# The second MLP's first layer in pairs of token tiles: 512-column products that share a PSUM bank, and the leaky step as a maximum

## The chip, the cores and the metric

The kernel runs on one core of one Trainium2 chip. Its time is the device time of one execution in microseconds. A core has a matrix engine (TensorE, PE; its weight loads are PEld), a vector engine (VectorE, DVE), an activation engine (ScalarE, ACT), a general engine (GpSimd, POOL) and a queue that issues the transfers (SyncE, SP). Each takes its instructions in order and waits on semaphores for the others. PE writes only to PSUM, which has 8 banks of 512 float32 columns by 128 partitions.

## The reference

Linear attention over `q`, `k`, `v` gives 4608 tokens of 512 features. Two MLPs follow, each 512 -> 2048 -> 512. The change is in the first layer of the second one and in its leaky step:

```python
h = x @ w_in                                            # first MLP, squared ReLU
r = np.maximum(h, 0.0)
x = (r * r) @ w_out
h = x @ w2_in                                           # (4608 x 512) @ (512 x 2048)
g = np.maximum(h, 0.0) + alpha * np.minimum(h, 0.0)     # alpha: one per column, 0 to 0.3
out = g @ w2_out
```

The weights come as 8-byte numbers; the kernel joins their halves into float32.

## The kernel before

The tokens are cut into 9 tiles of 512 (`T`). Four stages follow each other, each over all tiles: the attention with the first layer of MLP 1 (`hidden_stage`, line 756), its second layer (`project_stage`, line 793), the first layer of MLP 2 (`hidden_pairs`, line 900), its second layer (`project_stage` again). Between stages the tiles lie in device memory (`r_dram`, `y_dram`).

Every float32 operand is split into a rounded head (ACT, `split.head`, line 481) and the rest (DVE, `split.rest`, line 484), both of type fp32r, and a product is made of three matmuls: `PAIRS = ((1, 0), (0, 1), (0, 0))`. From the second stage on, a 2 x 2 block product is formed from seven block products instead of eight (a scheme of Strassen's kind in Winograd's form): sums of operand blocks are made first (`token_blocks`, lines 500, 506, 509; `Pairs.made` for the weights), and sums of the seven results afterwards. In `hidden_pairs` a group `g` is 256 of the 2048 hidden columns against one tile, whose 512 tokens are two halves of 256 (`HALF`). Each of its seven products (1, 3, 2, 6, 7, 5, 4) is six matmuls of 256 columns: two 128-row halves of the contraction (`c`) by three pairs. They land in the halves of four banks. `prelu` adds them up: ACT copies products 1 and 3 out of PSUM (line 928), DVE makes the sums (lines 932, 935, 938, 944), POOL one of them (941), and the leaky step is ReLU(-z) on ACT (947), its scaling by `-alpha` (952), and max(z, 0) plus that, on DVE (955) for even groups or on ACT and POOL (967, 968) for odd ones. A store to `r_dram` (972) follows.

The order on each engine is not the order of the code. `Plan` collects all operations with an engine, an assumed cost, what they come after, the buffers they take and a due time, and places them one by one: on each engine, the operation that can start soonest, and among those within `SLACK` of it the one due first. The result is a fixed order per engine. Buffers have fixed places (`homes`, in units of 256 words), and kinds whose places overlap share them in time: the loaded token blocks `ri` (14 to 35), results `o` (37 to 53), and `z`, `zt` of the leaky step.

Around the change: the last tile of the second stage ends with `combine` (lines 825 to 841), which adds its seven accumulated banks on ACT and DVE and stores them (`store_y`). The weights of `w2_in`, 8 groups, are brought back from device memory and split (768 and 1024 elements a group) as soon as the second stage's last tile frees their places, so partly after the third stage has begun. The weights of `w2_out` and the first token blocks of the last stage are made in the same way during the last tile of the third.

## Time and profile before

| what | value |
| --- | --- |
| median of 3 runs | 1626.44 us (1624.84 to 1627.63) |
| span of the profiled execution | 1623.9 us |
| time of the profiled execution | not recorded beside its span; the median of the runs lies 2.5 us above the span |
| third stage, starts of the first and the last L900 matmul | 881.4 and 1253.6 us |
| matmuls of the third stage | 3024 of 128x128 by 256 columns |
| DMA over the span | 176 GB/s |

The page counts busy time per engine, follows back the chain of work that ended last, and lists groups of instructions by source line with their mean duration and the idle time ahead of them. Matmuls overlap in the pipeline: the mean duration of one is longer than the distance from one to the next, so the distance is taken from stretches of the chain that hold many of them.

### The profile page before, as it was taken

The numbers are of one execution on the slowest core, as the hardware profiler recorded it, in microseconds if no ns is written. First come the engines' busy times: TensorE is split into PE (matmuls) and PEld (weight loads), VectorE is DVE, ScalarE is ACT, GpSimd is POOL, SyncE is SP. The second block draws the span as 40 slices with busy tenths as digits, with TensorE's granted clock in tenths as the row PEclk, the third lists the DMA queues.
The fourth block names the chain that finished last, engine by engine and source line by source line (L and its number), as shares of the span: only waits on it lengthen the run. The fifth ranks groups of instructions, "written<-read, shape, count | busy, mean of one in ns | idle before, by whom it ended". The sixth has DMA issues, their size and how long they took to land.

```text
span 1623.9 us, 30239 instructions
## 1 busy us (share of the span) xinstructions
PE 1583.6 (98%) x11840; PEld 1489.6 (92%) x11840; DVE 1214.4 (75%) x2108; ACT 963.3 (59%) x1500; POOL 276.1 (17%) x248
## 2 busy tenths in 40 slices
PE   5899999999999999999999899999999999999998
PEld 3678888888888999999999899999999999999998
DVE  7765767667626888888877977777769998888873
ACT  5677766766757544444444777787778644444442
POOL 4431111111100000000021333333333000000011
PEclk9999999999999999999999999999999999999999
DMA  8677788887657444444444433333346544444441
GB/s 218 193 224 270 240 265 262 282 289 269 243 207 272 151 142 140 137 129 135 133 151 158 163 131 131 130 143 135 133 165 215 189 150 151 133 145 133 131 120 64
DMA packets 125247, 287.19 MB, mean 177 GB/s; under 512 B 15024, under 2 KB 73392, under 8 KB 125104
## 3 DMA queue, kind: packets, MB, share of 16 engines
q1 hardware_dynamic: 125104, 285.26, 53.3%
q8 instruction: 92, 1.51, 0.4%
q14 instruction: 51, 0.42, 0.1%
HBM read 168.83 MB, written 116.39 MB: 176 GB/s over the span
## 4 chain that ended last, share of the span: by engine, by line
PE 89%; DVE 5%; DMA 2%; issue 2%; ACT 1%; POOL 1%; SPq 0%; DVEq 0%; POOLq 0%; ACTq 0%
PE bank L793 43%; PE bank L756 23%; PE bank L900 19%; DVE sr L484 2%; PE bank L590 1%; DMA sb<-in_moe_w_in_dram 1%; PE bank L664 1%; PE bank L736 1%; PE bank L679 1%; PE bank L680 1%; PE bank L678 0%; DMA sb<-in_k_dram 0%; DVE sb L500 0%; DVE sb L932 0%; POOL sr L397 0%
## 5 line engine op out<-in xcount | busy, mean ns | idle before, releaser
L793 PE MATMUL bank<-sr 128*128 128x256 f32 x6048 | 727.5, 283 | 0.9 <-DVE sb L832 0.7
L793 PEld LDWEIGHTS bank<-sr 128*128 128x128 f32 x6048 | 726.3, 192 | 2.0 <-DVE sb L832 0.9
L481 ACT CAST sr<-sb 128x512 fp32r<-128x512 f32 (+2 forms) x534 | 371.6, 713 | 366.5 <-PE bank L793 216.0
L484 DVE TENSOR_TENSOR sr<-sb,sr 128x768 fp32r<-128x768 f32 (+2 forms) x534 | 426.6, 824 | 107.8 <-ACT sr L481 106.9
L756 PE MATMUL bank<-sr 128*128 128x512 f32 x1680 | 406.5, 397 | 5.8 <-POOL sr L397 5.8
L756 PEld LDWEIGHTS bank<-sr 128*128 128x128 f32 x1680 | 311.8, 189 | 72.5 <-POOL sr L397 7.4
L900 PE MATMUL bank<-sr 128*128 128x256 f32 x3024 | 366.4, 284 | 5.5 <-DVE sr L484 4.0
L900 PEld LDWEIGHTS bank<-sr 128*128 128x128 f32 x3024 | 364.9, 193 | 6.9 <-DVE sr L484 5.3
L506 POOL TENSOR_TENSOR sb<-sb 128x256 f32<-128x256 f32 x16 | 17.6, 1098 | 719.0 <-ACT sr L481 672.3
L784 ACT ACTIVATE sb<-bank 128x512 f32<-128x512 f32 x144 | 85.7, 595 | 76.7 <-PE bank L756 65.7
L500 DVE TENSOR_TENSOR sb<-sb 128x512 f32<-128x512 f32 x162 | 114.7, 710 | 3.3 <-DMA sb<-r 1.8
L968 POOL TENSOR_TENSOR sb<-sb 128x1024 f32<-128x1024 f32 x36 | 89.5, 2486 | 156.7 <-ACT sb L967 152.4
L947 ACT ACTIVATE sb<-sb 128x1024 f32<-128x1024 f32 x72 | 76.2, 1058 | 42.8 <-DVE sb L944 42.5
L832 DVE TENSOR_TENSOR sb<-sb,bank 128x512 f32<-128x512 f32 x108 | 71.1, 685 | 36.8 <-PE bank L793 17.1
L952 ACT ACTIVATE sb<-sb,al_neg 128x512 f32<-128x512 f32 x144 | 96.9, 717 | 2.2
L785 ACT ACTIVATE sb<-sb 128x512 f32<-128x512 f32 x144 | 91.0, 632 | 3.4
L932 DVE TENSOR_TENSOR sb<-bank,sb 128x512 f32<-128x512 f32 x72 | 49.4, 687 | 41.7 <-ACT sb L928 36.5
L660 POOL TENSOR_TENSOR sb<-sb 128x512 f32<-128x512 f32 x36 | 37.8, 1051 | 225.4 <-DVE sb L656 84.8
L941 POOL TENSOR_TENSOR sb<-sb 128x256 f32<-128x256 f32 x72 | 53.9, 750 | 104.4 <-DVE sb L932 100.0
L509 DVE TENSOR_TENSOR sb<-sb 128x256 f32<-128x256 f32 x146 | 64.3, 442 | 4.2
L938 DVE TENSOR_TENSOR sb<-bank,sb 128x512 f32<-128x512 f32 x72 | 49.8, 691 | 18.5 <-PE bank L900 13.1
L506 DVE TENSOR_TENSOR sb<-sb 128x256 f32<-128x256 f32 x146 | 63.0, 435 | 0.8
(67 smaller groups left out, 1055.5 us busy)
## 6 DMA issues: line engine op xcount, KB each, us to landing
r<-sb SPq DMA_DIRECT2D x144, 512.0 KB, 3.1
sb<-r SPq DMA_DIRECT2D x144, 512.0 KB, 3.7
j<-sb SPq DMA_DIRECT2D x24, 896.0 KB, 6.0
sb<-j SPq DMA_DIRECT2D x24, 896.0 KB, 5.0
sb<-in_moe_w_in_dram SPq DMA_DIRECT2D x32, 512.0 KB, 5.2
sb<-in_moe_w_out_dram SPq DMA_DIRECT2D x32, 512.0 KB, 4.9
y_scratch<-sb SPq DMA_DIRECT2D x36, 256.0 KB, 2.8
sb<-y_scratch SPq DMA_DIRECT2D x18, 512.0 KB, 4.9
```

The costliest lines, as they stand in the source:

```text
L481: nc.scalar.copy(of(parts.ap[:, :n]), what())
L484: nc.vector.tensor_tensor(of(parts.ap[:, n:]), what(), of(parts.ap[:, :n].bitcast(F32)), op=ALU.subtract)
L500: nc.vector.tensor_tensor(two(block(4, 2)), two(block(1, 2)), block(0).unsqueeze(1).to_broadcast([P, 2, HALF]), op=ALU.subtract)
L506: e.tensor_tensor(block(6), block(2), block(4), op=ALU.add)
L756: nc.tensor.matmul(h.ap, w[:, a, c, :], x_parts(x[c][0])[:, b, :], start=(c == 0 and n == 0), stop=(c == KB - 1 and n == 2),)
L784: o = plan.add(lambda: nc.scalar.activation(ro.ap[:, half], h.ap, AF.Relu), "act", 0.6, [o, even], new=new, use=[h, ro])
L785: return plan.add(lambda: nc.scalar.activation(ro.ap[:, half], ro.ap[:, half], AF.Square), "act", 0.63, [o], use=[ro])
L793: nc.tensor.matmul(target[:, m * HALF:(m + 1) * HALF], one[:, u, ms], two[:, w, :], start=start and m == 0 and i == 0, stop=stop and m == ...
L900: nc.tensor.matmul(h.ap[:, at * HALF:(at + 1) * HALF], a[:, u, c * P:(c + 1) * P], b[:, w, :], start=(m == 0 and c == 0 and z == 0), stop= ...
L947: nc.scalar.activation(zt.ap, block(0, 4), AF.Relu, scale=-1.0)
L952: nc.scalar.mul(half, half, al_neg[:, f:f + 1])
L968: o = plan.add(lambda: nc.gpsimd.tensor_tensor(block(0, 4), block(0, 4), zt.ap, op=ALU.add), "pool", 2.3, [o], use=[z, zt])
```

## The change

The third stage is `hidden_wide` instead of `hidden_pairs`. Eight of the nine tiles are taken in pairs, so that a block of tokens is a whole tile (512 columns, one bank) and the two blocks of a product are the two tiles; the ninth tile is taken alone with 256 columns as before. Each of the seven operands of a tile pair has a buffer of its own (`xt`, 14 in all: seven for each half of the contraction) and is made by one ACT copy and one DVE subtraction (`operand`, lines 924 to 928 of the new code). Two groups of weights are worked on together, their products alternating.

Products 1, 6, 7 and 4 add up in one bank: between them ACT copies the running sum out (`copy`, lines 1031 to 1042), and the next product goes on adding only after that. Product 2 has a bank, and 5 and 3 share one; DVE adds these to the copies (`plus`). The leaky step is one DVE operation, max(alpha * z, z) (`leak`), for alpha up to 1. For larger alphas `sign` turns the column round, and the rows of `w2_out` are turned back when they are joined (`rebias_by`). POOL has no part in the stage any more. `y_dram` is written so that a block of a tile pair can be read in pieces of 512.

```diff
-    al_neg = const.tile([P, NF], F32, name="al_neg")
+    sign = const.tile([P, NF], F32, name="sign")
+    rebias_by = const.tile([P, NF], F32, name="rebias_by")
...
-        z=kind(5 * HALF, 3, homes=homes(28, 5, 3)), zt=kind(4 * HALF, 2, homes=homes(43, 4, 2)),
+        xr=kind(7 * BANK, 2, homes=homes(14, 14, 2)), xt=kind(2 * BANK, 14, area=1, homes=homes(112, 4, 14)),
+        z=kind(2 * BANK, 8, homes=homes(49, -4, 2) + homes(8, -4, 3) + homes(38, -4, 7)),
...
-            nc.scalar.activation(high, high, AF.Prelu, scale=2.0 ** -112, alpha=-(2.0 ** 32))
+            scale = rebias_by[:, f:f + 1] if signed else 2.0 ** -112
+            nc.scalar.activation(high, high, AF.Prelu, scale=scale, alpha=-(2.0 ** 32))
...
+    def wide_blocks(load, after, n):
...
+        def operand(p, i, o):
+            x = buf(K["xt"])
+            operands[p] = x
+            o = plan.add(lambda: nc.scalar.copy(x.ap[:, :n], block(i)), "act", act_us(n), [o], new=[x], use=[j])
+            done[p] = plan.add(
+                lambda: nc.vector.tensor_tensor(x.ap[:, n:2 * n], block(i), x.ap[:, :n].bitcast(F32), op=ALU.subtract),
+                "dve", dve_us(n), [o], use=[x, j], lock=True,
+            )
...
+        sums = plan.add(t13, "dve", dve_us(2 * n), [loaded], use=[j], lock=True)
+        operand(1, 1, loaded)
+        operand(2, 3, loaded)
...
+    def hidden_wide(weights, y_done, r, gate):
...
+            for g in range(0, G, 2):
+                both = [Group(weights, xs, t, first, n, g + m, r) for m in range(2)]
+                for m, p in ((0, 1), (1, 1), (0, 2), (0, 6), (1, 6), (1, 2), (0, 5), (0, 7), (1, 7), (1, 5), (0, 4), (1, 4), (0, 3), (1, 3)):
+                    last[t, g + m] = both[m].product(p)
...
+            read = {6: 1, 7: 6, 4: 7, 3: 5}.get(p)
+            us = MM if n == BANK else MM2
+            o = product_op(
+                unit, 6 * us / MM, [self.weights.done[g][s], *(x[1][p] for x in self.xs), self.ends.get(read)],
+                new=[h] if start else [], use=[h, wb, *(x[0][p] for x in self.xs)],
+            )
...
+            def copy(to, by):
+                nc.scalar.mul(to, h.ap[:, :n], sign[:, by])
+
+            def plus(to, by):
+                nc.vector.scalar_tensor_tensor(to, h.ap[:, :n], sign[:, by], to, op0=ALU.mult, op1=ALU.add)
+
+            def leak(to, by):
+                nc.vector.scalar_tensor_tensor(to, to, al[:, by], to, op0=ALU.mult, op1=ALU.max)
...
-    h2, r2 = hidden_pairs(w2i, y_done, r_dram[1], lambda t, h2: p1[T - 1, 3, 5] if t == 0 else h2[t - 1, 1])
+    h2, r2 = hidden_wide(w2i, y_done, r_dram[1], lambda t, h2: p1[T - 1, 3, 5] if t == 0 else h2[t - 1, 3])
```

How the change moves instructions shows at three places. First PE where the second stage ends and the third begins; `bank5_70` and `bank3_68` hold products of the last tile of the second stage (L793 before, L796 now), six matmuls a row. Before:

```order
L793 MATMUL bank6_71<-sr_64 128x256 x6
L793 MATMUL bank2_67<-sr_64 128x256 x6
L793 MATMUL bank5_70<-sr_64 128x256 x6
L900 MATMUL bank4_69<-sr_64 128x256 x6
L793 MATMUL bank3_68<-sr_64 128x256 x6
L900 MATMUL bank7_72<-sr_64 128x256 x6
L900 MATMUL bank4_69<-sr_64 128x256 x6
L900 MATMUL bank7_72<-sr_64 128x256 x6
L900 MATMUL bank0_65<-sr_64 128x256 x6
L900 MATMUL bank1_66<-sr_64 128x256 x6
```

Now, from the same product on:

```order
L796 MATMUL bank6_71<-sr_64 128x256 x6
L796 MATMUL bank2_67<-sr_64 128x256 x6
L796 MATMUL bank5_70<-sr_64 128x256 x6
L796 MATMUL bank3_68<-sr_64 128x256 x6
L983 MATMUL bank4_69<-sr_64 128x512 x6
L983 MATMUL bank7_72<-sr_64 128x512 x6
L983 MATMUL bank0_65<-sr_64 128x512 x6
L983 MATMUL bank4_69<-sr_64 128x512 x6
L983 MATMUL bank1_66<-sr_64 128x512 x6
L983 MATMUL bank6_71<-sr_64 128x512 x6
L983 MATMUL bank7_72<-sr_64 128x512 x6
L983 MATMUL bank4_69<-sr_64 128x512 x6
```

The one product of the third stage that stood ahead of the second stage's last (product 5) is gone from there. The third stage begins behind it, and its products of two groups alternate; a bank comes back after two to four others.

Second, DVE at the same place. L832 before and L835 now are the additions of `combine`, which wait for PE's last products; L484 and L487 are `split.rest`; in the new code L895, L901 and L904 are the sums of token blocks and L911 is the DVE half of an operand. Before:

```order
L832 TENSOR_TENSOR sb_63<-sb_63,bank0_65 128x512
L832 TENSOR_TENSOR sb_63<-sb_63,bank6_71 128x512
L841 TENSOR_TENSOR sb_63<-sb_63 128x512
L832 TENSOR_TENSOR sb_63<-sb_63,bank2_67 128x512
L832 TENSOR_TENSOR sb_63<-sb_63,bank5_70 128x512
L484 TENSOR_TENSOR sr_64<-sb_63,sr_64 128x768
L832 TENSOR_TENSOR sb_63<-sb_63,bank3_68 128x512 x2
L932 TENSOR_TENSOR sb_63<-bank7_72,sb_63 128x2x256
L935 TENSOR_TENSOR sb_63<-bank0_65,sb_63 128x256
L484 TENSOR_TENSOR sr_64<-sb_63,sr_64 128x1024
```

Now:

```order
L835 TENSOR_TENSOR sb_63<-sb_63,bank0_65 128x512
L835 TENSOR_TENSOR sb_63<-sb_63,bank6_71 128x512
L844 TENSOR_TENSOR sb_63<-sb_63 128x512
L835 TENSOR_TENSOR sb_63<-sb_63,bank2_67 128x512
L835 TENSOR_TENSOR sb_63<-sb_63,bank5_70 128x512
L911 TENSOR_TENSOR sr_64<-sb_63,sr_64 128x512
L895 TENSOR_TENSOR sb_63<-sb_63 128x1024
L911 TENSOR_TENSOR sr_64<-sb_63,sr_64 128x512
L901 TENSOR_TENSOR sb_63<-sb_63 128x512
L911 TENSOR_TENSOR sr_64<-sb_63,sr_64 128x512
L835 TENSOR_TENSOR sb_63<-sb_63,bank3_68 128x512
L911 TENSOR_TENSOR sr_64<-sb_63,sr_64 128x512
```

The block sums of the second half of the contraction (the second L895) and the first operand made from it (the L911 behind it) stand behind four additions of `combine` and the sum of two of its results (L844).

Third, PE at the end of the third stage. Before, the products of the last stage (L793) follow those of the third:

```order
L900 MATMUL bank6_71<-sr_64 128x256 x6
L900 MATMUL bank1_66<-sr_64 128x256 x6
L900 MATMUL bank6_71<-sr_64 128x256 x6
L900 MATMUL bank3_68<-sr_64 128x256 x6
L900 MATMUL bank4_69<-sr_64 128x256 x12
L793 MATMUL bank5_70<-sr_64 128x256 x6
L793 MATMUL bank7_72<-sr_64 128x256 x6
L793 MATMUL bank0_65<-sr_64 128x256 x6
```

Now one product of the last stage (L796) stands ahead of the last seven products of the third:

```order
L983 MATMUL bank7_72<-sr_64 128x256 x6
L796 MATMUL bank6_71<-sr_64 128x256 x6
L983 MATMUL bank3_68<-sr_64 128x256 x6
L983 MATMUL bank5_70<-sr_64 128x256 x6
L983 MATMUL bank3_68<-sr_64 128x256 x6
L983 MATMUL bank5_70<-sr_64 128x256 x6
L983 MATMUL bank3_68<-sr_64 128x256 x6
L983 MATMUL bank1_66<-sr_64 128x256 x6
L983 MATMUL bank7_72<-sr_64 128x256 x6
L796 MATMUL bank2_67<-sr_64 128x256 x6
L796 MATMUL bank0_65<-sr_64 128x256 x6
```

## Rows read from the trace of the kernel before

**Rows 1.** The page: span, and PE's busy time with its share and instructions

```profile
span 1623.9 us, 30239 instructions
...
PE 1583.6 (98%) x11840; PEld 1489.6 (92%) x11840; DVE 1214.4 (75%) x2108; ACT 963.3 (59%) x1500; POOL 276.1 (17%) x248
```

**Rows 2.** The page: the chain that ended last, by engine and line

```profile
PE 89%; DVE 5%; DMA 2%; issue 2%; ACT 1%; POOL 1%; SPq 0%; DVEq 0%; POOLq 0%; ACTq 0%
```

**Rows 3.** Busy time, the third stage: PE, PEld, DVE, ACT, POOL, clock, DMA

```profile
934.00:1243.00 309.00, 308.94 (x2575) 308.74 (x2573) 224.58 (x371) 237.40 (x329) 119.04 (x91) 1.00 0.39 144
```

**Rows 4.** The chain in order of time: start, length, what, instructions

```profile
49.87 2.75 PE bank L756 x12
...
473.21 46.24 PE bank L756 x204
...
916.03 10.38 PE bank L900 x72
932.25 271.85 PE bank L900 x2262
```

**Rows 5.** PE in order of time, second stage into third; idle ahead in brackets

```profile
882.16 0.88 PE L793 MATMUL bank<-sr 128*128 128x256 f32 x6
...
916.03 14.08 PE L900 MATMUL bank<-sr 128*128 128x256 f32 x103 [3.18 <-DVE sr L484]
930.36 1.31 PE L900 MATMUL bank<-sr 128*128 128x256 f32 x6 [0.24 <-DVE sr L484]
932.25 12.98 PE L900 MATMUL bank<-sr 128*128 128x256 f32 x104 [0.58 <-DVE sr L484]
```

**Rows 6.** Busy time and granted clock of PE alone, 916 to 922 us

```profile
916.00:918.00 2.00, 1.97 (x9) 0.50 0.20 82
...
920.00:922.00 2.00, 2.00 (x19) 1.00 0.32 129
```

**Rows 7.** PE in order of time, third stage into fourth

```profile
1244.31 9.61 PE L900 MATMUL bank<-sr 128*128 128x256 f32 x78 [1.36 <-DVE sb L932]
...
1297.65 2.53 PE L793 MATMUL bank<-sr 128*128 128x256 f32 x19 [0.69 <-DVE sb L832]
```

**Rows 8.** DVE in order of time, around 1240 us

```profile
1240.73 2.92 DVE L500 TENSOR_TENSOR sb<-sb 128x512 f32<-128x512 f32 x1
1243.57 0.68 DVE L932 TENSOR_TENSOR sb<-bank,sb 128x512 f32<-128x512 f32 x1
```

**Rows 9.** POOL in order of time, around 1240 us

```profile
1240.70 2.41 POOL L968 TENSOR_TENSOR sb<-sb 128x1024 f32<-128x1024 f32 x1 [4.38 <-ACT sb L967]
```

**Rows 10.** Groups by line and shape, whole run, DVE and ACT: busy, mean ns

```profile
L484 DVE TENSOR_TENSOR sr<-sb,sr 128x512 fp32r<-128x512 f32 x324 | 222.0, 699 | 52.2 <-ACT sr L481 51.7
...
L484 DVE TENSOR_TENSOR sr<-sb,sr 128x768 fp32r<-128x768 f32 x186 | 182.7, 987 | 49.7 <-ACT sr L481 49.3
...
L952 ACT ACTIVATE sb<-sb,al_neg 128x512 f32<-128x512 f32 x144 | 96.9, 717 | 2.2
L785 ACT ACTIVATE sb<-sb 128x512 f32<-128x512 f32 x144 | 91.0, 632 | 3.4
...
L932 DVE TENSOR_TENSOR sb<-bank,sb 128x512 f32<-128x512 f32 x72 | 49.4, 687 | 41.7 <-ACT sb L928 36.5 <-PE bank L900 3.5 <-issue 1.6
...
L928 ACT COPY sb<-bank 128x512 f32<-128x512 f32 x72 | 41.3, 573 | 35.7 <-PE bank L900 30.2 <-POOL sb L968 3.1 <-DMA r<-sb 1.2
...
L935 DVE TENSOR_TENSOR sb<-bank,sb 128x256 f32<-128x256 f32 x72 | 30.5, 424 | 6.9 <-PE bank L900 0.5 <-POOL sb L968 0.2
...
L484 DVE TENSOR_TENSOR sr<-sb,sr 128x1024 fp32r<-128x1024 f32 x24 | 29.8, 1242 | 5.9 <-ACT sr L481 5.9
```

**Rows 11.** DVE in order of time, the second stage's end

```profile
880.98 0.69 DVE L841 TENSOR_TENSOR sb<-sb 128x512 f32<-128x512 f32 x1
881.78 1.48 DVE L832 TENSOR_TENSOR sb<-sb,bank 128x512 f32<-128x512 f32 x2
```

**Rows 12.** The page: transfers of y, KB each, us from issue to landing

```profile
y_scratch<-sb SPq DMA_DIRECT2D x36, 256.0 KB, 2.8
```

More of the change, by code (lines that the diff above doesn't have):

```diff
@@ L879, in store_out, with block, t13, t2 @@
         )
-    def hidden_pairs(weights, y_done, r, gate):
+    WIDE = [(t, BANK) for t in range(0, T - 1, 2)] + [(T - 1, HALF)]
+    def wide_blocks(load, after, n):
+        j = buf(K["xr"])
+        operands, done = {}, {}
+        def block(i, many=1):
+            return j.ap[:, i * n:(i + many) * n]
+        def t13():
+            nc.vector.tensor_tensor(
+                block(4, 2).rearrange("p (i n) -> p i n", i=2), block(1, 2).rearrange("p (i n) -> p i n", i=2),
+                block(0).unsqueeze(1).to_broadcast([P, 2, n]), op=ALU.subtract,
+            )
+        def t2():
+            nc.vector.tensor_tensor(block(6), block(2), block(4), op=ALU.add)
+        def t4():
+            nc.vector.tensor_tensor(block(0), block(3), block(6), op=ALU.subtract)
+        def operand(p, i, o):
[6 more added lines that the diff above has]
+            )
+        loaded = None
+        for h in range(2):
+            loaded = plan.add(
+                lambda h=h: load(block(0, 4).rearrange("p (k h t) -> p k h t", k=2, h=2)[:, :, h], h), "sp", ISSUE,
+                [*after, loaded], new=[] if h else [j], use=[j], mb=n / 1000,
+            )
+        sums = plan.add(t13, "dve", dve_us(2 * n), [loaded], use=[j], lock=True)
+        operand(1, 1, loaded)
+        operand(2, 3, loaded)
+        o = plan.add(t2, "dve", dve_us(n), [sums], use=[j], lock=True)
+        operand(6, 6, o)
+        operand(5, 4, sums)
+        operand(7, 5, sums)
+        o = plan.add(t4, "dve", dve_us(n), [o], use=[j], lock=True)
+        operand(4, 0, o)
+        operand(3, 2, loaded)
+        return operands, done
@@ L883, in hidden_pairs @@
+    def hidden_wide(weights, y_done, r, gate):
         last, stored = {}, {}
[L884 removed]
+        for t, (first, n) in enumerate(WIDE):
             xs = []
             for c in range(2):
[L887 to L911 removed]
@@ new lines, in load @@
+                def load(to, h, c=c, first=first, n=n):
+                    if n == BANK:
+                        y = y_dram[first + h].rearrange("p (k c h) t -> p k c (h t)", c=2, h=2)
+                        nc.sync.dma_start(to, y[:, :, c])
+                    else:
+                        y = y_dram[first].rearrange("p (k c h) t -> p k c h t", c=2, h=2)
+                        nc.sync.dma_start(to, y[:, :, c, h])
+                ys = [y_done[t2, i, j] for t2 in range(first, first + n // HALF) for i in (1, 2) for j in (1, 2)]
@@ new lines, in hidden_wide @@
+                xs.append(wide_blocks(load, [*ys, gate(t, last)], n))
+            for g in range(0, G, 2):
+                both = [Group(weights, xs, t, first, n, g + m, r) for m in range(2)]
+                for m, p in ((0, 1), (1, 1), (0, 2), (0, 6), (1, 6), (1, 2), (0, 5), (0, 7), (1, 7), (1, 5), (0, 4), (1, 4), (0, 3), (1, 3)):
+                    last[t, g + m] = both[m].product(p)
+                for m in range(2):
+                    for h in range(2):
+                        for t2 in range(first, first + n // HALF) if n == HALF else [first + h]:
+                            stored.setdefault((t2, g + m), []).append(both[m].stored[h])
```

172 lines of the change are left out of this document (86 added, 86 removed).

## The prediction

> **What bounds the kernel now.** I read the page first: PE is busy for 98% of the span [rows 1], and the chain that ended last is PE for 89% [rows 2]. Then the stretch of the third stage that lies free of its two ends: PE is busy for 308.94 of 309.00 us, while DVE has 224.6 (73%), ACT 237.4 (77%) and POOL 119.0 us (39%) [rows 3]. So in the middle of the stage nothing but PE's own pace counts, and a change of ACT's or DVE's work is worth nothing there by itself. The pace is in the chain in order of time [rows 4]: 2262 matmuls of 256 columns in 271.85 us, 0.1202 us from one to the next, and in the first stage 204 of 512 columns in 46.24 us, 0.2267 us. Both ran at the full granted clock. Two of 256 columns take 0.2404, one of 512 takes 0.2267: 0.0137 us is what a matmul costs beside its columns.
>
> At the ends PE waits. In order of time [rows 5] the second stage goes over into the third without a gap; then PE stands idle for 3.18 us before 916.03, and for 0.24 and 0.58 us soon after, each time for DVE's L484, the second half of a weight split. After the 3.18 us the granted clock was 0.50, half of 2.4 GHz, and full again by 920 [rows 6]; the 72 matmuls behind the gap took 10.38 us [rows 4] instead of 72 x 0.1202 = 8.65, so 1.73 us more. Two gaps of 1.36 and 0.69 us lie at the change to the fourth stage [rows 7]. The 1.36 us comes at the end of a DVE addition of 2.92 us [rows 8] that lay beside a POOL operation of 2.41 us [rows 9]; alone such an addition takes about 0.69.
>
> **The change, part by part.** *Matmuls.* Before: 3024 x 0.1202 = 363.4 us. Now four tile pairs x 8 groups x 42 = 1344 of 512 columns and 8 x 42 = 336 of 256: 1344 x 0.2267 + 336 x 0.1202 = 304.7 + 40.4 = 345.1 us. That is 18.3 us less. The rows give 0.2292 as the other end for 512 columns (12 in 2.75 us, an isolated product with its end [rows 4]); with it 3.4 us of the gain are lost. I take 0.2267, since products follow each other closely here as in the long row.
>
> On this term one rule stands against the trace. The Trainium skill (TensorE: Matmul & The Clock Gate, "Wait — 56ns, not 53.3ns?") gives the distance of warm matmuls as columns over 2.4 GHz and a fixed 2.5 ns; it was measured on another type. By it 1344 matmuls fewer would save 1344 x 2.5 ns = 3.4 us. The rows here show 13.7 ns and decide.
>
> *The late weights.* Groups of weights were used up every 42 x 0.1202 = 5.05 us, and DVE, which splits them, fell behind. A pair of groups now lasts 84 x 0.2267 = 19.0 us. The waits of 3.18 + 0.24 + 0.58 = 4.0 us and the 1.73 us at the low clock should go. Bounds: nothing to all of it stays. DVE's work in a wide tile: 8 groups x 7 operations on 512 columns (3 `plus`, 4 `leak`) x 0.687 = 38.5 us by L932; 14 operands x 0.699 = 9.8 by L484; sums 2 x (1.242 + 2 x 0.687) = 5.2; together 53.5 us [rows 10] beside 8 x 42 x 0.2267 = 76.2 us of PE. In the first tile up to 8 x (0.987 + 1.242) = 17.8 us of weight splits come on top: 71.3 of 76.2. It fits, closely, and by the order of DVE two of the eight groups and a part of the third are split before the stage begins.
>
> *A new wait at the stage's first product.* Product 1 needs operands of both halves of the contraction. In the order of DVE the second half's sum (second L895) and its first operand (L911) stand behind the additions of `combine`, of which the last needs product 4. In the trace that pair of additions began at 881.78, right behind L841, and lasted 1.48 us [rows 11], so to 883.26. Behind it come L911, L895 and L911: 0.70 + 1.24 + 0.70, less 0.08 us each by which an instruction starts before the one ahead of it ends (1243.57 against 1240.73 + 2.92 [rows 8]): to about 885.66. PE would be through with the second stage at 882.16, since the six matmuls ahead of its last product [rows 5] are gone. That is 3.5 us idle where there was none; 2.8 if an addition comes sooner, 4.5 if the operand's data or a semaphore is later. It is as long as the gap of 3.18, so I add the same loss at the low clock, 1.7 us (0 to 3.4). The seventh product is (group 1, 6): it waits for a copy into a place that a result of `combine` held. DVE's last addition for that ends near 889.1 (885.66 and five operations), its store lands 2.8 us later [rows 12], the copy takes 0.66: 892.6, and the product's turn is 885.66 + 6 x 1.36 = 893.8. I cost it at nothing, with 1.2 us to spare.
>
> *Reading a bank and adding on in it.* This happens four times a group (before products 6, 7, 4, 3), 160 times in all. A copy with a scale from memory is not in the trace from PSUM; the copy L928 takes 0.573, and a scale from memory makes L952 0.717 against 0.632 for L785, so 0.573 + 0.085 = 0.66 us (0.57 to 0.72) [rows 10]. Two products, 2.72 us, stand between product 1 and product 6 of a group, and two or more before each of the others, so the copy has three times the time it needs. In the ninth tile the cover is 12 x 0.1202 = 1.44 us. ACT's work falls to about 32 x 0.66 + 14 x 0.63 = 30 us of 76. All of this lies behind PE. If the cover were gone, each of the 160 would cost what it lacks.
>
> *The end of the stage.* POOL has no work there now, so the stretched addition and its 1.36 us should go. But the ninth tile is as dense for DVE as before (14 x 0.424 = 5.9 us [rows 10] for 10.1 us of PE, with the splits for the last stage beside it), and the places of its results must be stored before they come round. Of the 1.36 + 0.69 us I keep 0.9 (0 to 4).
>
> *Small parts.* Sixteen weight chunks of `w2_out` get 0.085 us more on ACT in the first stage, 1.4 us in all under PE's products; three tiny DVE operations replace one; a few transfers more on SP, of y in pieces of 1 KB instead of 2 KB, a stage ahead of their use. Nothing; without that cover it would be 1 to 2 us.
>
> *Sum.* -18.3 - (4.0 + 1.7) - (1.36 + 0.69) + 3.5 + 1.7 + 0.9 = -20.0 us against the profiled span of 1623.9: 1603.9. The page gives that execution no time beside its span; the runs' median, 1626.4, lies 2.5 above it. With these: 1606.4 us.
>
> **The rivals.** *DVE falls behind where tiles change.* The 14 operand buffers hold one tile pair, so the next pair's operands can be made only as the last two groups let go of them, product by product. In those 19.0 us DVE has 9.6 us of its usual work and up to 15.0 of operands and sums: 24.6. For it: DVE fell behind at 913 us under a similar burst. Against it: products let go in the order in which the next tile asks, 2.7 us apart, so half of the burst may lie in the next 19 us. If a third to a half of the excess of 5.6 us shows at each of the four changes, 2 us each: 1606.4 + 8 = 1614.
>
> *The reads hold up PE; this is the slower end.* Place: the products 6, 7, 4 and 3 of every group, behind ACT's in-order queue. If a copy finds two or three casts ahead of it (0.63 each, a weight split of 1024 over 1 us), its 0.9 us from product to reading becomes 2.9, 0.2 more than the cover: 160 x 0.2 = 32 us, 1638. From 20.0 / 160 = 0.125 us a time the gain is gone, from 0.146 the kernel is slower by over 0.2%. For it: L932 waited 36.5 us in all for the copy L928 [rows 10]. Against it: ACT has 39% to do instead of 77%, and the copies have the casts' turns to themselves outside the tile changes.
>
> *The fixed part of a matmul does not shrink.* If what a matmul costs beside its columns grew with them in this stage, the first term would fall to a few us. If 512 columns cost 0.2377 us here, so that a fifth of the 0.0137 is left of each pair, 1344 x 0.0027 = 3.7 us of the 18.3 remain, and the time is 1606.4 + 14.6 = 1621. (The Trainium skill's rule above would come to nearly that.) For it: no row shows 512 columns in this stage. Against it: the same operand types, line by line the same form, ran at 0.2267 for 46 us.
>
> **How the numbers follow.** Forecast 0.77 (its own range 1603 to 1610: the gain at the start's shorter end, or the slower 512 and some of the old waits), DVE at the tile changes 0.14, the reads 0.06, the fixed part 0.03. The range 1602 to 1613 leaves out about 0.15, mostly the last two and the upper half of the second. What a measurement of this kernel can tell from no change is about 0.2%, 3.3 us. Faster by more: all but the reads and a little else, 0.91; within: 0.04, a mild form of the reads; slower: 0.05.
>
> **What would show it.** Right: the third stage's matmuls of 512 columns 0.227 us apart over long stretches; one idle time of 3 to 4 us at the stage's first product, released by L911, with the granted clock at half behind it; no waits for weight splits; PE without gaps between tile pairs; about 350 us from the stage's first product to its last. Wrong: idle PE ahead of products 6, 7, 4, 3 with ACT as releaser; gaps at the four tile changes with L911 as releaser; a distance over 0.230 us.

## The result, and the profile after

The changed kernel takes 1603.44 us, median of 4 runs (1600.01 to 1603.62). The kernel before, run beside it, takes 1625.64 (1623.99 to 1627.63). The ratio is 0.9864, with a 95% interval of 0.9849 to 0.9878: 22.2 us faster. Forecast were 1606.4 us and a range of 1602 to 1613. A second set of 4 runs gave 1600.93 (1599.40 to 1601.95), ratio 0.9856 [0.9841, 0.9870].

The page of the changed kernel, beside [rows 1, 2]: PE has 1344 matmuls fewer and keeps its 98%, and the chain is PE for 94% instead of 89%. ACT has gone from 963 to 829 us and POOL from 276 to 134.

```profile
span 1601.7 us, 27016 instructions
...
PE 1563.7 (98%) x10496; PEld 1418.2 (89%) x10496; DVE 1193.0 (74%) x2058; ACT 829.2 (52%) x1352; POOL 133.9 (8%) x140
...
PE 94%; DMA 2%; DVE 2%; issue 1%; POOL 1%; ACT 1%; SPq 0%; DVEq 0%; POOLq 0%
...
L983 PE MATMUL bank<-sr 128*128 128x512 f32 (+1 forms) x1680 | 346.4, 368 | 2.1 <-ACT sr L909 1.3
```

The chain of the changed kernel in order of time (start, length, what, instructions), beside [rows 4]. Where there were several pieces with gaps, the third stage's part is now one long piece of PE, 888.21 to 1214.41. From there to 1228.15 the chain runs mostly over DVE, though PE itself works on until 1227.79, as the rows of PE below show:

```profile
522.00 360.73 PE bank L796 x3006
...
888.21 326.20 PE bank L983 x1525
...
1234.43 362.41 PE bank L796 x3018
```

PE of the changed kernel in order of time at the stage's two ends, beside [rows 5, 7] (in brackets the idle time ahead and its releaser). At the start there are two idle times, 1.32 and 0.83 us, with four matmuls of 512 columns run before they are over. At the end one of 0.36 us is left, and none at the change to the fourth stage:

```profile
884.71 0.86 PE L983 MATMUL bank<-sr 128*128 128x512 f32 x3
886.89 0.49 PE L983 MATMUL bank<-sr 128*128 128x512 f32 x1 [1.32 <-ACT sr L909]
888.21 339.58 PE L983 MATMUL bank<-sr 128*128 128x512 f32 x1634 [0.83 <-DVE sr L911]
1228.15 0.98 PE L796 MATMUL bank<-sr 128*128 128x256 f32 x6 [0.36 <-DVE sr L487]
1228.97 5.46 PE L983 MATMUL bank<-sr 128*128 128x256 f32 x42
1234.26 5.92 PE L796 MATMUL bank<-sr 128*128 128x256 f32 x48
```

Busy time of the changed kernel (PE, PEld, DVE, ACT, POOL; then granted clock, DMA share, GB/s), beside [rows 3, 6]. PE is never idle from 934 to 1227, and all four tile changes lie in that stretch (at about 964, 1040, 1116 and 1192). One wide tile (961 to 1037) leaves DVE a quarter of its time. Behind the idle times at the start the clock is full:

```profile
888.00:890.00 2.00, 1.79 (x8) 1.50 (x9) 2.00 (x5) 1.52 (x4) 0.00 (x0) 1.00 0.00 0
...
934.00:1227.00 293.00, 293.00 (x1429) 248.54 (x1428) 212.81 (x327) 119.24 (x197) 0.00 (x0) 1.00 0.39 146
...
961.00:1037.00 76.00, 76.00 (x337) 62.96 (x336) 55.33 (x79) 29.91 (x47) 0.00 (x0) 1.00 0.36 139
```

From here on stages are compared, since the first stage ends at another time in each execution (the second stage's long row begins at 517 to 524 us, whatever is changed behind it). Third stage: its first matmul to the fourth stage's first, less 0.72 us for each moved product that belongs to a neighbour. Fourth: the rest of the span. All from one profiled execution each, in us:

| kernel | third stage | fourth | second stage's start to the end |
| --- | --- | --- | --- |
| before | 371.6 | 370.0 | 1104.5 |
| changed | 348.8 | 368.0 | 1079.7 |
| changed, second set | 348.8 | 368.0 | 1079.7 |

The two executions of the changed kernel agree to 0.1 us, although one of its second stages began 1.6 us earlier than the other. So the change is worth 24.8 us behind the first stage: 22.8 in the third stage and 2.0 in the fourth. The span shows 22.2, since the second stage began at 522.00 instead of 519.45 in this execution.

### The profile page after: what moved, and what is told of

Same layout as the page of the kernel before. It is cut to its first block, busy times and chain, and to the rows that moved or that the text cites. A ratio compares the mean times of both kernels' runs of the same rounds, so it can differ in the third digit from the quotient of the medians.

```text
span 1601.7 us, 27016 instructions
## 1 busy us (share of the span) xinstructions
PE 1563.7 (98%) x10496; PEld 1418.2 (89%) x10496; DVE 1193.0 (74%) x2058; ACT 829.2 (52%) x1352; POOL 133.9 (8%) x140
## 4 chain that ended last, share of the span: by engine, by line
PE 94%; DMA 2%; DVE 2%; issue 1%; POOL 1%; ACT 1%; SPq 0%; DVEq 0%; POOLq 0%
PE bank L796 45%; PE bank L759 23%; PE bank L983 21%; PE bank L593 1%; DMA sb<-in_moe_w_in_dram 1%; PE bank L667 1%; DMA sb<-in_k_dram 1%; PE bank L739 1%; PE bank L682 1%; PE bank L683 1%; PE bank L681 0%; POOL sr L400 0%; DMA sb<-in_q_dram 0%; DVE sr L487 0%; DVE sb L1011 0%
## 5 line engine op out<-in xcount | busy, mean ns | idle before, releaser
L796 PE MATMUL bank<-sr 128*128 128x256 f32 x6048 | 726.6, 283 | 0.4 <-DVE sr L487 0.4
L796 PEld LDWEIGHTS bank<-sr 128*128 128x128 f32 x6048 | 726.1, 192 | 0.8 <-DVE sr L487 0.6
L484 ACT CAST sr<-sb 128x512 fp32r<-128x512 f32 (+2 forms) x480 | 337.1, 718 | 357.6 <-PE bank L796 212.7
L487 DVE TENSOR_TENSOR sr<-sb,sr 128x512 fp32r<-128x512 f32 (+2 forms) x480 | 380.7, 818 | 108.8 <-ACT sr L484 107.6
L759 PEld LDWEIGHTS bank<-sr 128*128 128x128 f32 x1680 | 312.1, 190 | 72.3 <-POOL sr L400 7.1
L983 PE MATMUL bank<-sr 128*128 128x512 f32 (+1 forms) x1680 | 346.4, 368 | 2.1 <-ACT sr L909 1.3
L983 PEld LDWEIGHTS bank<-sr 128*128 128x128 f32 x1680 | 293.0, 188 | 55.3 <-ACT sr L909 1.8
L1005 ACT ACTIVATE sb<-bank,sign 128x512 f32<-128x512 f32 (+1 forms) x160 | 103.4, 648 | 194.9 <-PE bank L983 190.2
L1011 DVE SCALAR_TENSOR_TENSOR sb<-sb,al 128x512 f32<-128x512 f32 (+1 forms) x160 | 110.0, 697 | 11.4 <-ACT sb L1005 8.0
L509 POOL TENSOR_TENSOR sb<-sb 128x256 f32<-128x256 f32 x16 | 16.7, 1045 | 1097.8 <-ACT sr L484 1060.3
L835 DVE TENSOR_TENSOR sb<-sb,bank 128x512 f32<-128x512 f32 x108 | 71.3, 686 | 35.1 <-PE bank L796 15.4
L1008 DVE SCALAR_TENSOR_TENSOR sb<-bank,sign,sb 128x512 f32<-128x512 f32 (+1 forms) x80 | 55.5, 694 | 41.8 <-PE bank L983 39.6
L689 DVE TENSOR_TENSOR sr<-bank,sr 128x512 fp32r<-128x512 f32 x36 | 24.8, 690 | 37.2 <-ACT sr L686 36.9
L566 DVE TENSOR_REDUCE sb<-sb 128x128 f32<-128x640 f32 x32 | 41.6, 1301 | 9.4 <-DMA sb<-in_k_dram 7.0
L1035 DVE SCALAR_TENSOR_TENSOR sb<-bank,sign,sb 128x512 f32<-128x512 f32 (+1 forms) x40 | 27.7, 697 | 27.8 <-ACT sb L1005 20.2
```

The source lines that it names most:

```text
L484: nc.scalar.copy(of(parts.ap[:, :n]), what())
L487: nc.vector.tensor_tensor(of(parts.ap[:, n:]), what(), of(parts.ap[:, :n].bitcast(F32)), op=ALU.subtract)
L509: e.tensor_tensor(block(6), block(2), block(4), op=ALU.add)
L759: nc.tensor.matmul(h.ap, w[:, a, c, :], x_parts(x[c][0])[:, b, :], start=(c == 0 and n == 0), stop=(c == KB - 1 and n == 2),)
L796: nc.tensor.matmul(target[:, m * HALF:(m + 1) * HALF], one[:, u, ms], two[:, w, :], start=start and m == 0 and i == 0, stop=stop and m == ...
L835: lambda: nc.vector.tensor_tensor(c.ap, b.ap, acc[p].ap, op=ALU.add), "dve", 0.7,
```

## The experiments

### Half the columns, twice the matmuls

The changed kernel, each 512-column matmul as two of 256:

```diff
-                        nc.tensor.matmul(
-                            h.ap[:, :n], a[:, u, c * P:(c + 1) * P], b[:, w, :n],
...
+                        for s in range(0, n, HALF):
+                            nc.tensor.matmul(
+                                h.ap[:, s:s + HALF], a[:, u, c * P:(c + 1) * P], b[:, w, s:s + HALF],
...
```

> The changed kernel, each 512-column matmul issued as two of 256 columns (1344 more matmuls, all else the same: order of products, buffers, copies). Theory (each matmul costs 0.0137 us beside its columns, and that is the larger part of the gain): the third stage grows by 1344 x 0.0137 = 18.4 us, from 349.7 to about 368, matmuls 0.120 us apart, time about 1622. Rival (the gain comes from the fewer waits and the other order of work, not from the number of matmuls): within 3 us of the changed kernel, about 1603 to 1606.

Measured: 1620.59 us, ratio to before 0.9978 [0.9969, 0.9987]. The third stage takes 367.7 us, 18.8 more than in the changed kernel; 0.77 of that is a wait near its end that was not there. Its PE in order of time:

```profile
884.48 0.50 PE L984 MATMUL bank<-sr 128*128 128x256 f32 x2 [1.30 <-ACT sr L909]
885.80 357.40 PE L984 MATMUL bank<-sr 128*128 128x256 f32 x2974 [0.82 <-DVE sr L911]
...
1245.33 5.51 PE L984 MATMUL bank<-sr 128*128 128x256 f32 x42 [0.77 <-ACT sb L1006]
```

The waits at the start are as in the changed kernel and the middle has no gap, so 18.1 us is what the 1344 further matmuls cost: 0.0134 us each. So the third rival, that the fixed part doesn't shrink, falls. Each further matmul has a weight load of its own (11840 matmuls and 11840 loads, against 10496 of each), so the run does not tell whether the matmul or its load costs the 0.0134 us.

### The leaky step alone

The kernel before, with the maximum on DVE in place of four or five operations on ACT, DVE and POOL:

```diff
-        o = plan.add(below, "act", 1.04, [o, o3], use=[z, zt])
...
+        def leak(m):
+            f = 2 * g + m
+            nc.vector.scalar_tensor_tensor(block(2 * m, 2), block(2 * m, 2), al[:, f:f + 1], block(2 * m, 2), op0=ALU.mult, op1=ALU.max)
...
```

> The kernel before with the leaky step alone changed: two maximum operations of 512 columns on DVE a group in place of ReLU, two scalings and the last sum on ACT, POOL and DVE. Theory (ACT, POOL and DVE lie under PE in the middle of the stage): nothing there; at the end of the stage the wait of 1.36 us beside POOL's long addition goes; DVE gets 1.8 us more a pair of groups (some 3.3 less the 1.2 of the old sum and a saved share), so the waits at the stage's start stay or grow a little. Time 1623 to 1628, no change that counts. Rival (freeing ACT and POOL is a good part of the 22 us): 8 us or more faster, 1618 or less.

Measured: 1620.22 us, ratio 0.9981 [0.9972, 0.9990]. It is 3.9 us faster than the kernel before, which neither the theory (no change that counts) nor its rival (8 us or more) had. The three waits of 3.18, 0.24 and 0.58 us [rows 5] are one of 0.89, and the 1.36 us [rows 7] are gone. PE in order of time:

```profile
925.97 321.27 PE L900 MATMUL bank<-sr 128*128 128x256 f32 x2669 [0.89 <-DVE sr L484]
1247.08 44.44 PE L793 MATMUL bank<-sr 128*128 128x256 f32 x348
1292.21 8.06 PE L793 MATMUL bank<-sr 128*128 128x256 f32 x65 [0.69 <-DVE sb L832]
```

The third stage takes 364.8 us instead of 371.6. So the late weights were not only a matter of how fast groups are used up; something that the leaky step put on ACT, DVE or POOL made them late.

### Half the weight splits

The kernel before, with groups 4 to 7 multiplying by the split weights of groups 0 to 3, so that half the splits fall away (the output is then computed with those weights):

```diff
+                if n == 1 and g >= G // 2:
+                    self.blocks.append(self.blocks[g - G // 2])
...
```

> The kernel before, in which groups 4 to 7 of the third stage use the split weights of groups 0 to 3, so that four groups of weights are neither brought back nor split at the start of the stage (the results of those columns are left wrong). Theory (the waits of 3.18, 0.24 and 0.58 us and the 1.7 us at the low clock come from these splits): they go, 5.7 us less in the third stage, time about 1620. Rival (DVE is behind there for the tokens' and the results' work, and the weights only happen to be what PE waits for): the gaps shrink by half at most and the third stage loses 3 us or less.

Measured: 1614.93 us, ratio 0.9953 [0.9939, 0.9966]. The third stage is one row without a gap, and takes 362.9 us, 8.7 less than before:

```profile
887.10 362.32 PE L905 MATMUL bank<-sr 128*128 128x256 f32 x3018
```

The splits are needed for the waits, as expected. The 1.36 us at the end went with them, which was not; that the places left free let the next weights in earlier is a guess that no run here tests. With 8.7 us the whole of what PE lost in the stage is found: 371.6 less 3024 x 0.1202 = 363.4 is 8.2, and this run's own row has a pace of 0.1201.

### No POOL in the leaky step

Which engine's relief was it? The kernel before, with the last step on DVE for odd groups as well, which gives DVE more work, not less. POOL's addition goes from 36 groups, and with it an ACT operation of about 1 us:

```diff
-        if g % 2:
+        if g < 0:
```

> The kernel before with the last step of the leaky function done on VectorE for all groups, as it was for the even ones: GpSimd's addition of 2.4 us and ScalarE's operation of 1 us go from 36 groups, and VectorE gets one of 1.25 us more in each. With the leaky step as two maxima on VectorE alone the kernel before became 5.4 us faster, and its waits at the third stage's start shrank from 4.0 to 0.9 us. Theory A: that relief came from GpSimd, whose additions stretch VectorE's (2.92 us instead of 0.69 beside one). Then it returns here although VectorE has more to do: the 1.36 us wait at the stage's end goes, the waits at the start shrink to about 1 us with no low clock behind, and the time is 3 to 6 us below the kernel before. Theory B: it came from having less to do on ScalarE and VectorE: VectorE is fuller here by 36 x 1.25 = 45 us, so the waits at the start stay or grow: no change or up to 5 us slower.

Measured: 1619.26 us, ratio 0.9971 [0.9960, 0.9981]. The waits at the start are 1.02 and 0.58 us and the 1.36 is gone; the third stage takes 367.0 us, 4.6 less than before, with DVE's added work in it. The low clock did not go with them: it is 0.50 (third from the end of the last row) behind these two shorter waits, which theory A had not expected:

```profile
880.48 42.54 PE L900 MATMUL bank<-sr 128*128 128x256 f32 x349
924.04 0.62 PE L900 MATMUL bank<-sr 128*128 128x256 f32 x3 [1.02 <-DVE sr L484]
925.24 321.66 PE L900 MATMUL bank<-sr 128*128 128x256 f32 x2666 [0.58 <-DVE sr L484]
1246.74 43.55 PE L793 MATMUL bank<-sr 128*128 128x256 f32 x348
...
926.00:928.00 2.00, 2.00 (x11) 2.00 (x11) 1.95 (x3) 0.46 (x1) 1.47 (x1) 0.50 0.00 0
```

In its main point theory A holds: it was POOL. ACT's relief does not explain it, since ACT is nearly as busy over 884 to 935 us as before (36.4 against 37.7 us) and DVE waits for it longer, not shorter (1.7 us ahead of L932 against 0.3). The kernel before shows how. DVE's instructions one by one, just ahead of the 3.18 us, and the mean of all 8 weight splits of 768 elements over 884 to 935 (in the last column but one), here and then in the run without POOL:

```profile
898.81 0.41 DVE L944 TENSOR_TENSOR sb<-bank,sb 128x256 f32<-128x256 f32 x1
899.23 2.56 DVE L484 TENSOR_TENSOR sr<-sb,sr 128x768 fp32r<-128x768 f32 x1
...
903.44 0.95 DVE L484 TENSOR_TENSOR sr<-sb,sr 128x768 fp32r<-128x768 f32 x1
...
911.98 3.13 DVE L484 TENSOR_TENSOR sr<-sb,sr 128x768 fp32r<-128x768 f32 x1
...
L484 DVE TENSOR_TENSOR sr<-sb,sr 128x768 fp32r<-128x768 f32 x8 | 11.2, 1422 | 0.0
...
L484 DVE TENSOR_TENSOR sr<-sb,sr 128x768 fp32r<-128x768 f32 x7 | 6.7, 950 | 0.0
```

and POOL of the kernel before in the same stretch:

```profile
898.55 2.42 POOL L968 TENSOR_TENSOR sb<-sb 128x1024 f32<-128x1024 f32 x1 [1.65 <-ACT sb L967]
...
911.36 2.93 POOL L968 TENSOR_TENSOR sb<-sb 128x1024 f32<-128x1024 f32 x1 [1.01 <-ACT sb L967]
```

A split of 768 elements alone takes 0.95 us. The one at 899.23 takes 2.56, 1.61 too long, and POOL's addition covers its first 1.74 us (899.23 to 900.97). The one at 911.98 takes 3.13, 2.18 too long. Each ends 0.82 us after POOL's addition, at 901.78 and 915.11, so the split stands still while that addition runs: 3.8 us lost in two splits, ahead of a wait of 3.18. The addition at 898.81, with one of its inputs in PSUM, takes its usual 0.41 us beside the same POOL operation. The Trainium skill has the rule (SBUF — State Buffer, "Who interferes with whom": VectorE and GpSimd share a pair of ports as an exclusive lock, and a VectorE `tensor_tensor` with both inputs in SBUF contends with GpSimd's reads); the trace agrees, with 1.61 us lost for 1.74 covered, and 2.18 for 2.31. The prediction had seen this for the 1.36 us [rows 8, 9], and not looked for it ahead of the 3.18.

### One group at a time

The changed kernel with the order 1, 2, 6, 5, 7, 4, 3 of one group after another, every product held behind the one before it, and the fourth stage's first products behind the third's last (that part of the edit is not shown):

```diff
-                for m, p in ((0, 1), (1, 1), (0, 2), (0, 6), (1, 6), (1, 2), (0, 5), (0, 7), (1, 7), (1, 5), (0, 4), (1, 4), (0, 3), (1, 3)):
+                for m, p in [(m, p) for m in range(2) for p in (1, 2, 6, 5, 7, 4, 3)]:
...
```

> The changed kernel with the products of one group finished before the next group begins (order 1, 2, 6, 5, 7, 4, 3), so that nothing stands between products 7 and 4, which follow each other in one PSUM bank with a copy by ScalarE between them. Theory: the copies of the bank cost TensorE nothing in the changed kernel only because other products lie between. Then each product 4 now waits for a whole copy: its measured 0.69 us and about 0.1 us on either side for the signals, 0.9 us. 32 groups in the wide tiles at 0.9 us and 8 in the ninth at 0.7 us are about 34 us, so near 1638 us, with idle TensorE ahead of product 4 released by ScalarE. The pairs 1 to 6 and 6 to 7 have one product of 1.36 us between them and should show nothing. Rival: the copies are short beside the pipeline of matmuls and do not hold TensorE at all: within 3 us of the changed kernel's 1603.4 us.

Measured: 1666.54 us, ratio 1.0262 [1.0245, 1.0280]; the third stage takes 414.0 us, 65.2 more than in the changed kernel. In the wide tiles there is one wait a group, ahead of product 4, and the groups follow each other every 10.63 us instead of 42 x 0.2267 = 9.52. One of them in order of time (the row runs from product 4 to the next group's), a tile change, and two waits of the ninth tile:

```profile
913.16 9.86 PE L987 MATMUL bank<-sr 128*128 128x512 f32 x42 [0.78 <-ACT sb L1011]
...
981.53 6.20 PE L987 MATMUL bank<-sr 128*128 128x512 f32 x26 [0.59 <-DVE sr L913]
...
1263.22 1.65 PE L987 MATMUL bank<-sr 128*128 128x256 f32 x6 [3.73 <-ACT sb L1011]
...
1282.31 1.43 PE L987 MATMUL bank<-sr 128*128 128x256 f32 x6 [2.44 <-ACT sb L1011]
```

The mechanism is as expected and the price a little higher: 1.11 us a read instead of 0.9, 35.5 us for 32 groups. The other 30 are 4.7 at the start (a wait of 3.25 us for a DVE reading at 902.29), 0.9 at each of three tile changes, and some 22 in the ninth tile, where 5.6 had been expected (8 reads at 0.7): products of 0.72 us cover less there, waits of 2.44 and 3.73 us stand, and the granted clock is 0.50 behind the longest. The reads cost nothing in the changed kernel because a second group's products lie between; the prediction's second rival describes a mechanism that exists, and the order of the products keeps it away.

### Twice the leaky step

```diff
-                nc.vector.scalar_tensor_tensor(to, to, al[:, by], to, op0=ALU.mult, op1=ALU.max)
+                for _ in range(2):
+                    nc.vector.scalar_tensor_tensor(to, to, al[:, by], to, op0=ALU.mult, op1=ALU.max)
```

> The changed kernel with the leaky maximum issued twice on VectorE (the second changes columns of negative values again, so the numbers differ where h is negative). It asks how much room VectorE had. In the second, third and fourth wide tile of the changed kernel VectorE was busy for about 55 of 76 us; 32 more operations of 0.75 us, less 0.08 us of overlap each, make 21 us: 76.6 of 76.2. In the first tile with its weight splits 64.4 + 21.4 = 86 of 76, in the ninth tile and behind it, where it was busy for 38.8 of 45 us, some 13 us more. Theory (TensorE is held up as soon as VectorE's work in a stretch exceeds TensorE's, as feared for the tile changes): about 10 us at the first tile, little at the next three, about 8 at the ninth: 15 to 25 us slower, near 1622, idle TensorE from the middle of the first tile on. Rival: the buffers and the idle time spread it out: within 3 us of the changed kernel.

Measured: 1636.84 us, ratio 1.0079 [1.0064, 1.0094]; 35.9 us over the changed kernel of the same call, where 15 to 25 were expected. Busy time of one wide tile in it (DVE is the third pair), from one wait to the same wait of the next tile, and PE in order of time:

```profile
1048.48:1129.24 80.76, 77.48 (x336) 62.68 (x336) 76.35 (x109) 29.10 (x47) 0.00 (x0) 1.00 0.34 131
```

```profile
1048.48 1.66 PE L983 MATMUL bank<-sr 128*128 128x512 f32 x6 [0.27 <-DVE sb L1036]
1051.31 17.99 PE L983 MATMUL bank<-sr 128*128 128x512 f32 x78 [1.17 <-DVE sb L1036]
...
1129.24 1.66 PE L983 MATMUL bank<-sr 128*128 128x512 f32 x6 [0.27 <-DVE sb L1036]
```

PE is held up in every wide tile: the pattern of waits at 1048 comes again at 1129.24, 80.8 us later instead of 76.2. The work was sized rightly: DVE is busy for 76.35 us in that period, where 76.6 had been expected beside PE's 76.2. But "little at the next three" tiles was wrong: a tile loses 4.6 us, not 0.4, since DVE in turn stands idle for 4.4 of the 80.8. The releaser is the reading of product 5's bank (L1036), which product 3 adds on to; that its turn in DVE's fixed order makes it late is read from this and not tested. The limit lies between 55 and 76 us of DVE work for a tile of 76.2; at 55 there was no gap.

### The late half first

The order of the two halves of the contraction inside a product turned round:

```diff
-                for c in range(2):
+                for c in (1, 0):
...
```

> The changed kernel with the two halves of the contraction taken in the other order inside each product, so that the third stage's first product begins with the half whose operand is made last, and waits for it as a whole. In the changed kernel three matmuls of the early half and one of the late half ran inside the 3.5 us between the second stage's end and the last matmul's operand, and the granted clock stayed full. Theory A: these 0.9 us of work are lost (idle in one piece of about 3.5 us instead of two of 1.3 and 0.8), and in addition the granted clock falls to half behind the unbroken idle time, as it did behind 3.18 us in the kernel before, for 1.7 us more: 2.6 us longer, about 1606. Theory B: the clock stays full behind 3.5 us of idle time too: 0.9 us longer, about 1604.3, and the row of the granted clock reads 1.00 right behind the gap.

Measured: 1603.39 us (1599.99 to 1604.86), which shows no difference from 1603.44, with executions of one kernel up to 5 us apart. The profiled execution does: the third stage, counted from the second stage's end, takes 352.4 us, 3.5 more, and its second stage had begun 3.5 us earlier (518.51 instead of 522.00), which hides it in the span. PE in order of time, and busy time with the granted clock (third from the end), which was 1.00 until 884:

```profile
883.40 0.49 PE L983 MATMUL bank<-sr 128*128 128x512 f32 x1 [2.02 <-ACT sr L909]
884.73 343.13 PE L983 MATMUL bank<-sr 128*128 128x512 f32 x1637 [0.83 <-DVE sr L911]
...
884.00:886.00 2.00, 1.27 (x3) 1.08 (x4) 2.00 (x5) 1.44 (x2) 0.00 (x0) 0.51 0.02 6
```

Idle in two pieces of 2.02 and 0.83 us with one matmul between, the clock fell to half until past 890; with 1.32 and 0.83 and four matmuls it stayed full. Theory A is what the trace shows, though the idle time did not come in one piece, and with 3.5 us where 2.6 were expected: three matmuls fewer inside the wait are 3 x 0.2267 = 0.7, so the low clock took 2.8 instead of 1.7. In the time it isn't resolved.

### One load step, and a later gate

In the changed kernel the second half's first operand is late since its token block's two transfers are placed as two steps. With both in one step:

```diff
-        for h in range(2):
-            loaded = plan.add(
+        def halves():
+            for h in range(2):
+                load(block(0, 4).rearrange("p (k h t) -> p k h t", k=2, h=2)[:, :, h], h)
...
```

> The changed kernel, in which both loads of a tile pair's half of the contraction are one step of the plan, the second no longer held back until the first has landed. In DVE's fixed order the second half's sum and its first operand then stand ahead of the additions of products 7 and 4 of the second stage. Theory (the 2.6 us lost at the first product come from that place in DVE's order): DVE reaches that sum at about 884.3 instead of 886.3, the first product's second half can start 2.0 us sooner, the loss at the stage's start falls to about 0.7 us, time about 1601.4. Rival (the operand waits for its data or for ACT): no change, 1603.4.

Measured: 1603.48 us, ratio 0.9876 [0.9863, 0.9890]: no gain. The wait at the start fell from 2.6 to 0.4 us in all (idle 0.22), but the order at the stage's end came out otherwise, with five waits that had not been there; from the second stage's start to the end its profiled execution takes 1082.1 us, 2.4 more than the changed kernel's. The largest two:

```profile
882.85 331.38 PE L982 MATMUL bank<-sr 128*128 128x512 f32 x1568 [0.22 <-DVE sr L911]
...
1235.03 3.29 PE L796 MATMUL bank<-sr 128*128 128x256 f32 x24 [1.71 <-DVE sr L487]
1240.05 0.98 PE L982 MATMUL bank<-sr 128*128 128x256 f32 x6 [1.73 <-ACT sb L1004]
```

The theory of the start holds, and that of the time falls. So the gate of the fourth stage's first loads was moved as well:

```diff
-    project_stage(r_dram[1], r2, w2o, False, store_out, h2[end, 0])
+    project_stage(r_dram[1], r2, w2o, False, store_out, h2[end, 2])
```

> The changed kernel with both transfers of a token block issued as one step, as in the earlier run that took the wait at the stage's start from 2.6 to 0.2 us but gained five waits (4.4 us in all) at its end, and with the fourth stage's first token blocks loaded only after group 2 of the ninth tile instead of group 0. Theory: the waits at the end come from the fourth stage's blocks being made on VectorE and ScalarE among the ninth tile's additions; with the later gate they lie behind them, and the gain at the start is kept: about 2 us below the changed kernel, 1601 to 1602. Rival: the work only moves on, and the waits come back at the fourth stage's first products: 1603 to 1605.

> The changed kernel once more, beside the next one on the same chip: 1603.4 us, third stage 349 us, as the control of the next.

> The version with one load step and the later gate, whose third stage lasted 345.5 us instead of 349.0, once more beside the changed kernel. Theory: the 3.5 us less at the two ends of the stage, less the 0.69 us wait that it has in the fourth stage, show in the time: 2 to 3 us below the changed kernel of the same call. Rival: the fourth stage gives it back: no difference over 1 us.

Measured: 1601.45 us, ratio to the kernel before 0.9858 [0.9844, 0.9871]. Run beside the changed kernel it takes 1600.35 us (1598.30 to 1602.30), ratio to the kernel before 0.9857 [0.9840, 0.9873], and the changed kernel 1600.93 (1599.40 to 1601.95). So the 2 to 3 us of the last theory did not come; the rival's "no difference over 1 us" did. PE of the second execution in order of time:

```profile
882.03 344.37 PE L982 MATMUL bank<-sr 128*128 128x512 f32 x1676 [0.22 <-DVE sr L911]
1226.23 43.35 PE L796 MATMUL bank<-sr 128*128 128x256 f32 x348
1270.28 59.90 PE L796 MATMUL bank<-sr 128*128 128x256 f32 x497 [0.69 <-DVE sb L835]
```

The third stage takes 345.5 us in both executions, with next to nothing left to gain: 345.1 is the sum of its matmuls. But the fourth takes 370.1, 2.1 more than in the changed kernel, with the 0.69 us of [rows 7] back. Of 3.3 us won, 1.2 are left from the second stage's start to the end (1078.5 against 1079.7), and the times of four runs each do not show so little. Both versions beat the kernel before; between them this is a tie in time.

## Why the prediction was right, and where its terms were off

The forecast came true, 3 us too high; the second set's 1600.93 us lies 1.1 below the range. That it came so close is in part luck. The change is worth 24.8 us behind the first stage, where the forecast's sum was 20.0. Of these 4.8 us, 2.55 are hidden by the second stage's later start in the profiled execution; 0.7 comes on top, since that execution's time lies 1.8 us above its span and not 2.5. Against the 24.8 us:

| term | predicted | measured | from |
| --- | --- | --- | --- |
| fewer matmuls | -18.3 | -18.1 | matmuls of half the size |
| late weights and low clock behind them | -5.7 | -5.7 | no such rows in the trace after |
| wait at the first product, and low clock | +3.5 +1.7 | +2.6 +0 | 3.50 us, less four matmuls of 0.2267 |
| idle at the third stage's end | -1.36 +0.9 | -1.36 +1.1 | 348.8 less 345.1 and 2.6; 0.36 of it is idle time |
| fourth stage | -0.69 | -2.0 | 370.0 to 368.0 |

They add up to -23.5 of the 24.8. Most of the other 1.3 us is a loss of before that the forecast left out: PE lost 8.2 us in that stage, of which the terms name 5.7 + 1.36 = 7.1.

*Matmuls.* Right, and on 0.0137 us each: the isolated product's 0.2292 was not needed. The fixed part that the Trainium skill gives for another type (TensorE: Matmul & The Clock Gate, "Wait — 56ns, not 53.3ns?", 2.5 ns) would have made 3.4 us of it; this kernel's matmuls show 13.4 ns each.

*The late weights.* Size right, reason incomplete. "Groups were used up every 5.05 us and DVE fell behind" names what DVE had to do, not why it didn't do it: two of its splits stood still beside POOL's additions, for 3.8 us. Taking POOL out of the step alone leaves 1.60 of the 4.0 us and a low clock behind them, and halving the splits alone leaves nothing. In the changed kernel both causes are weaker at once, POOL's gone and the groups slower. Whether wide tiles with POOL kept would still wait was not tried.

*The wait at the first product* is the step that failed. DVE's chain came as worked out: the two additions, L911, the second L895, L911.

```profile
884.33 1.48 DVE L835 TENSOR_TENSOR sb<-sb,bank 128x512 f32<-128x512 f32 x2
885.73 0.69 DVE L911 TENSOR_TENSOR sr<-sb,sr 128x512 fp32r<-128x512 f32 x1
886.33 1.22 DVE L895 TENSOR_TENSOR sb<-sb 128x1024 f32<-128x1024 f32 x1
887.47 0.69 DVE L911 TENSOR_TENSOR sr<-sb,sr 128x512 fp32r<-128x512 f32 x1
```

The operand was there 3.45 us after the second stage's end (884.71 to 888.16), and 3.5 was the forecast. But "product 1 needs operands of both halves" took the product as one unit. Its matmuls wait one by one: three use the first half alone, and a fourth only ACT's head of the second. They ran inside the wait, so 2.6 us were lost. The clock stayed full behind it, and the 1.7 us fell away; the run with the halves turned round shows that term, at 2.8 us. Why the clock held is not shown. That the four matmuls broke the idle time is not reason enough: in the run without POOL it fell to 0.50 behind 1.02 and 0.58 us with three matmuls between, which is less idle time than the 1.32 and 0.83 here.

*The reads and DVE at the tile changes.* Both rivals were real mechanisms with a price, and both stayed away. DVE's operations were longer than assumed (`plus` and `leak` 0.75 us instead of 0.687, ACT's copy 0.69 instead of 0.66), without a trace in the time. Groups by line, 884 to 1234 us:

```profile
L1011 DVE SCALAR_TENSOR_TENSOR sb<-sb,al 128x512 f32<-128x512 f32 x128 | 95.4, 751 | 10.5 <-ACT sb L1005 7.6
L1008 DVE SCALAR_TENSOR_TENSOR sb<-bank,sign,sb 128x512 f32<-128x512 f32 x64 | 47.8, 748 | 39.6 <-PE bank L983 37.6 <-ACT sr L909 1.9
...
L1005 ACT ACTIVATE sb<-bank,sign 128x512 f32<-128x512 f32 x128 | 88.4, 691 | 176.9 <-PE bank L983 176.8
```

*The fourth stage* was costed by its one visible gap, 0.69 us. It became 2.0 us shorter. The later gate brought the gap and 2.1 us back, so it seems to hang on how far the fourth stage's first blocks are made ahead, which no run varies alone. The 1.3 us beside the gap lie in the stage's first 348 matmuls, which take 43.35 us with the later gate (43.20 before) instead of 348 x 0.1202 = 41.8, in losses too small to be listed as waits.

## What to carry to other kernels

Where PE is without gaps, count matmuls: what each costs beside its columns is read from two rows of the same trace with different widths, and halving their number by doubling the columns paid 0.0134 us for each one saved, where the rows had said 0.0137. A wait is costed by the instruction, not by the step of the program that issues it: the part of a product that is ready runs inside the wait. Whether the clock falls behind a broken wait could not be told from the idle times here. When an engine is late, look whether its operations ahead of the wait are longer than their usual mean before counting its work; here the excess lay in two splits of DVE beside two additions of POOL. Take such a mean from single instructions: a row of a merged timeline names one shape for all that it holds.

## What was not expected of the hardware

- A weight split of 0.95 us took 2.56 beside a POOL addition of 2.42, another 3.13 beside one of 2.93, and each ended 0.82 us after that addition. An addition with one input in PSUM kept its 0.41 us there. Without POOL's additions the mean of the splits fell from 1.42 to 0.95 us.
- The granted clock fell to 0.51 behind idle times of 2.02 and 0.83 us with one matmul of 512 columns between them, and to 0.50 behind 1.02 and 0.58 with three of 256 between. It stayed at 1.00 behind 1.32 and 0.83 with one of 512 between and three ahead.
- On DVE a `scalar_tensor_tensor` of 512 elements with a scalar per partition from memory took 0.75 us, a `tensor_tensor` 0.69. On ACT a copy from PSUM with a scale from memory took 0.69, the plain one 0.57. In both pairs the instruction differs too, so the price of the scalar alone is not shown.
